# Attention units of 128 instead of 96 tokens, and a first MoE in six blocks of 512 tokens

## Chip, cores and metric

The kernel runs on one core of a Trainium2 chip. The metric is the device time of the kernel in microseconds. The core has a matrix engine (TensorE, PE in the profile; its weight loads are PEld), VectorE (DVE), ScalarE (ACT), GpSimd (POOL) and SyncE (SP), which here issues every DMA. TensorE writes to PSUM only; VectorE and ScalarE read PSUM.

## The reference, cut to what matters

A chunked attention is followed by two feed-forward layers, all in float32. Queries come in chunks of 32; a chunk sees 8 memory keys and a window from 16 keys before it to 8 keys behind it, which makes 64 keys.

```
# q, k, v: (4, 8 heads, 768, 64); mem_k, mem_v: (4, 8, 8, 64)
for c in range(24):
    k_full = concat([mem_k, k[max(0, 32*c - 16):min(768, 32*c + 40)]])
    v_full = concat([mem_v, v[same window]])
    scores = q[32*c:32*c + 32] @ k_full.T / 8
    a = exp(scores - max(scores)); a = a / (sum(a) + 1e-9)
    out[32*c:32*c + 32] = a @ v_full
x = out as (3072 tokens, 512)
x = relu(x @ w_in)**2 @ w_out                        # first MoE: 512 -> 2048 -> 512
x = (silu(x @ w_gate) * (x @ w_val)) @ w_out2        # second MoE: 512 -> 1536 -> 512
```

## The kernel before

**Attention** is computed in 32 units of 96 tokens (three chunks), all eight heads of a unit at once. `at_load` brings q and k of a unit, `at_scores` makes 24 matmuls of 64 keys by 32 queries, each in a tile of 64 rows and 32 columns of TensorE's array: two rows of tiles for two heads, three columns of tiles for the three chunks. The scores lie in PSUM (`abank`, rows of 72 columns, because the third chunk's 64 keys begin 8 further on). VectorE takes the maximum, ScalarE the exponentials and their sums, VectorE divides and turns the probabilities with 32x32 transposes into `pT` (the unit's 128 keys by 96 queries for each head). `at_pv` multiplies: for each head the unit's v (128 keys by 64 columns) is the weight and `pT` the moving operand of 96 columns; even heads write the lower 64 PSUM partitions, odd heads the upper, so neighbours use the two 64-column halves of the array. A float32 matmul appears in the trace as two instructions, each with a weight load of its own. `at_split_x` splits the result into a high and a low part (`x`).

**The first four units** have another path: they are needed before anything else can run. Their softmax subtracts the maximum first (`at_sub_0`), the turning is done by TensorE (`at_turn_0`, L199) and the products with v are small ones of a single chunk and head (`at_pv_0`, L217; 24 matmuls a unit, each of 32 columns).

**The first MoE** runs over blocks of tokens, `BLOCKS = (4, 4, 5, 5, 5, 5, 4)` units, so of 384 or 480 tokens. In a block there are 16 steps `f`. In a step TensorE makes the hidden tile (`hidden_pe`, 12 matmuls with 128x128 weights and the block's tokens as columns, L373: high x high, high x low and low x high over four slices of 128) and, two steps later, the projection (`project_pe`, L417, 12 matmuls again). Between them ScalarE and VectorE take the ReLU, square it twice and make its low part (`relu`, `square`, `square_again`, `square_lo`). Hidden tiles alternate between two PSUM banks. The order on TensorE is hidden(f+2), projection(f), hidden(f+3), projection(f+1), and so on.

**Where the other work stands** is fixed by tables. A step has four slots, so before there are 448. Everything up to the last two steps of the first block is written out in `OPENING`, a list of letters and unit or step numbers (S scores, T turning, O products with v, x y w v the pieces of the first hidden tile, a b hidden, c d projection, L weight loads). Behind that, `UNIT_AT` says at which slot a unit's products with v stand; its other stages stand `UNIT_LAGS` slots after the products of the unit before, in the order load, scores, maximum, two halves of the exponentials, normalization, turning, load of v, rest of the turning. `PREP_AT` and `PREP_LAGS` do the same for 18 chunks of weights of the second MoE, which pass through ScalarE, VectorE and GpSimd and go back to DRAM. Engines and the SP queue work in this order, and an instruction that waits holds what stands behind it on its engine.

**The second MoE** (L607, L654) runs over the tokens in blocks of 512 columns and is reached when the first is done. Its lines are not touched.

Of the kernel before, what the change touches and what calls it, by code (L numbers as in the profile page):

```python
# [19 lines left out]
GQ = 96  # L20
GK = 128
NG = S // GQ
NGRP = B * NG
NH = 8
# [4 lines left out]
UNIT_AT = (  # L29
    65, 76, 90, 101, 114, 126, 138, 151, 164, 178, 190, 203, 215, 227, 240, 254, 267, 279, 291, 305, 321, 337,  # L30
    353, 369,
)
UNIT_LAGS = (-8, 0, 1, 2, 5, 5, 6, 7, 5)
PREP_LAGS = (-11, 0, 2, 2, 4, 7, 6, 9, 10, 11)
BLOCKS = (4, 4, 5, 5, 5, 5, 4)
# [4 lines left out]
PREP_AT = (77, 102, 132, 146, 158, 178, 196, 212, 226, 238, 260, 270, 287, 300, 324, 340, 352, 364)  # L40
# [4 lines left out]
GM = GK + NMEM  # L45
UK = NI * GM
UCOLS = UQ + UK + UV
UV0 = 3 * NI * D
WN = 64
WK = 72  # L50
# [7 lines left out]
PIECES = (((0, 0), (32, 32)), ((0, 32), (32, 64)), ((0, 64), (32, 96), (64, 32)))  # L58
# [17 lines left out]
def attention_moe_moe_kernel(ctx, tc, att, v0, w1, w2, out):  # L76
# [39 lines left out]
    probs = [ap.tile([GQ, NH, GQ], F32, name=f"prob{i}") for i in range(2)]  # L116
    pT = ap.tile([128, NH, GQ], F32, name="pT")

    blk0 = [sum(BLOCKS[:t]) for t in range(len(BLOCKS))]
    units = [(t, g) for t, n in enumerate(BLOCKS) for g in range(blk0[t], blk0[t] + n)]  # L120
    xt = {}
    rows = []
    st = [dict() for _ in units]

    def at_load(u):
        t, g = units[u]
        if u in EARLY:
            raw = early[EARLY.index(u)][:, 0:UQ + UK]
        else:
            raw = ap.tile([128, UQ + UK], F32, tag="qk", name="qk")  # L130
        st[u]["raw"] = raw
        sp.dma_start(out=raw, in_=att[g, :, 0:UQ + UK])

    def at_load_v(u):
        t, g = units[u]
        if t:
            v = ap.tile([128, UV], F32, tag="v", name="v", bufs=2)
            sp.dma_start(out=v, in_=att[g, :, UQ + UK:])
        else:
            v = first_v[u // 2][:, u % 2 * UV0:(u % 2 + 1) * UV0]  # L140
            sp.dma_start(out=v, in_=v0[g])
        st[u]["v"] = v

    def at_scores(u):

        t, g = units[u]
        s = st[u]
        raw = s.pop("raw")
        wide = t > 0
        o = s["s"] = rows[1] if wide else rows[u % 2][:, :, :, 0:WN]  # L150
        for i in range(NI):
            for c in range(3):
                for r in range(2):
                    half = slice(64 * r, 64 * r + 64)
                    k = UQ + i * GM + (0, 32, 72)[c]
                    b = 8 if wide and c == 2 else 0
                    pe.matmul(  # L157
                        o[32 * c:32 * c + 32, r, i, b:b + 64],
                        raw[half, i * GQ + 32 * c:i * GQ + 32 * c + 32],
                        raw[half, k:k + 64], start=True, stop=True, tile_position=(64 * r, 32 * c),  # L160
                    )
        if g % NG == 0:
            dve.memset(o[0:32, :, :, 0:LEFT], NEG)
        if g % NG == NG - 1:
            e = 64 if wide else 64 - NMEM
            dve.memset(o[64:96, :, :, e - RIGHT:e], NEG)
# [5 lines left out]
    def at_sub_0(u):  # L172
# [7 lines left out]
        if u == BLOCKS[0] - 1:  # L180
            dve.memset(rows[1][64:96, :, :, 0:NMEM], NEG)
# [22 lines left out]
    def at_pv_0(u):  # L204
        t, g = units[u]
        s = st[u]
        if t not in xt:
            xt[t] = [xp.tile([128, KD, NTM], R, tag=f"x{i}", name=f"x{i}") for i in range(2)]
        v = s["v"].rearrange("p (c j d) -> p c j d", c=3, d=D)
        o = hbank[1][:, 0:KD * GQ].rearrange("p (j q) -> p j q", q=GQ)  # L210
        s["o"] = o.rearrange("p (r i) q -> p r i q", r=2)
        for j in range(NI):
            for c in range(3):
# [13 lines left out]
    def at_exp(u, heads=range(NH)):  # L227
# [29 lines left out]
    def at_turn(u, chunks=range(3)):  # L257
# [10 lines left out]
    def at_turn_2(u):  # L268
        at_turn(u, range(2, 3))

    def at_pv(u):
        t, g = units[u]
        s = st[u]
        if t not in xt:
            xt[t] = [xp.tile([128, KD, NTM], R, tag=f"x{i}", name=f"x{i}") for i in range(2)]
        o = s["o"] = abank[:, :, NI * WK:NI * WK + KD // 2 * GQ].rearrange("p r (i k) -> p r i k", k=GQ)
        for h in range(NH):
            r = D * (h % 2)
            pe.matmul(  # L279
                o[r:r + D, h // NI, h % NI // 2], s["v"][:, h * D:(h + 1) * D], pT[:, h],  # L280
                start=True, stop=True, tile_position=(0, r),
            )

    def at_x(u):
        t, g = units[u]
        c = (g - blk0[t]) * GQ
        return [x[:, :, c:c + GQ].rearrange("p (r i) k -> p r i k", r=2) for x in xt[t]]

    def at_x_hi(u):
        act.copy(at_x(u)[0], st[u]["o"])  # L290

    def at_x_lo(u):
        hi, lo = at_x(u)
        dve.tensor_tensor(lo, st[u]["o"], hi.bitcast(F32), ALU.subtract)
        st[u].clear()

    def at_split_x(u):
        at_x_hi(u)
        at_x_lo(u)
# [7 lines left out]
    nunit = BLOCKS[0]  # L307
    before = -1
    for t, n in enumerate(BLOCKS[1:], 1):
        for j in range(n):  # L310
            e = 13 * j + 12 if t == 1 else UNIT_AT[nunit - 8]
            for lag, fn in STAGES:
                plan.setdefault(max(0, before + lag + (t == 2 and j == 0 and lag > 2)), []).append((lag, fn, nunit))
            plan.setdefault(e, []).append((100, at_pv, nunit))
            plan.setdefault(e + 1, []).append((101, at_split_x, nunit))
            before = e
            nunit += 1
# [7 lines left out]
    nt_of = [GQ * n for n in BLOCKS]  # L325
# [96 lines left out]
    def project(t, f, between):  # L422
# [5 lines left out]
        if f == NF1 - 1:  # L428
            t0 = blk0[t] * GQ
# [275 lines left out]
    for i in range(2):  # L705
        pool.memset(probs[i][:, :, WK:GQ], 0.0)
    for o in (yb0, abank):
        rows.append(o[0:GQ, :, 0:NI * WK].rearrange("p r (i k) -> p r i k", k=WK))
    dve.memset(rows[1], NEG)
# [22 lines left out]
    def side(hs):  # L732
# [15 lines left out]
        "O": lambda u: (at_pv_0 if u < BLOCKS[0] else at_pv)(u), "X": at_x_hi, "Y": at_x_lo, "F": at_exp_1,  # L748
# [6 lines left out]
        "M": lambda u: (at_max_0 if u < BLOCKS[0] else at_max)(u),  # L755
# [5 lines left out]
    early = [t[:, c:c + WC] for t in (rawp.tile([128, RAW], F32, tag="raw", name="early") for _ in range(2)) for c in (0, WC)]  # L761
# [110 lines left out]
def _pack(inputs):  # L872
# [8 lines left out]
    att = np.empty((NGRP, 128, UCOLS), q.dtype)  # L881
    for b in range(B):
        for g in range(NG):
            w0 = g * GQ
            win_k = np.concatenate([kp[b, :, w0:w0 + CHUNK], mk[b], kp[b, :, w0 + CHUNK:w0 + GK - NMEM]], axis=1)
            win_k = np.concatenate([win_k, mk[b]], axis=1)
            win_v = np.concatenate([vp[b, :, w0:w0 + CHUNK], mv[b], vp[b, :, w0 + CHUNK:w0 + GK - NMEM]], axis=1)
            a = att[b * NG + g]
            qT = q[b, :, w0:w0 + GQ].reshape(2, NI, GQ, D).transpose(0, 3, 1, 2)
            kT = win_k.reshape(2, NI, GM, D).transpose(0, 3, 1, 2)  # L890
            a[:, 0:UQ] = qT.reshape(128, UQ)
            a[:, UQ:UQ + UK] = kT.reshape(128, UK)
            a[:, UQ + UK:] = win_v.transpose(1, 0, 2).reshape(GK, UV)
    v0 = np.empty((BLOCKS[0], 2, WN, 3, NI, D), v.dtype)
    for g in range(BLOCKS[0]):
        rows = att[g, :, UQ + UK:].reshape(GK, NI, 2, D)
        for c, keys in enumerate((rows[0:64], rows[32:96], np.concatenate([rows[72:128], rows[32:40]]))):
            v0[g, :, :, c] = keys.transpose(2, 0, 1, 3)
    v0 = v0.reshape(BLOCKS[0], 128, UV0)
# [38 lines left out]
```

## Time and profile before

| | |
|---|---|
| median of 3 runs | 1133.77 us (1133.75 to 1133.96) |
| the profiled execution | 1131.54 us |
| its span, first to last instruction | 1129.8 us |
| TensorE busy | 1116.8 us, 99% of the span |
| VectorE, ScalarE, GpSimd busy | 705.6, 532.5, 317.5 us |
| granted clock, mean | 0.999 |

The span is what the trace shows; 1.7 us of the execution lie outside it. Busy time is the union of an engine's instructions. Matmuls are pipelined, so a busy TensorE isn't TensorE at its peak; how fast its stream runs is read from the times between instructions, which the chain shows as pieces. Times in the trace are in us from the span's start, and the trace lacks a few records of TensorE.

### The profile page before, as it was taken

To read this page: it belongs to the slowest core of one execution; us is meant where nothing else is said; L and a number is where in the kernel's file an instruction comes from. 1 tells how busy PE (TensorE), PEld (TensorE's weight loads), DVE (VectorE), ACT (ScalarE), POOL (GpSimd) and SP (SyncE) were. 2 spreads that over 40 slices of the span, in tenths; PEclk is the share of its full clock that TensorE was granted. 3 is DMA by queue.
4 is the path that set the end of the run, shared out by engine and by line. 5 is a ranking of instruction groups with operands and counts; after the bars stand their busy time and mean duration, and the time that the engine had idled before them with its cause. 6 is when DMAs were issued, how large, how long until landed. Compare 5 with 4: busy or idle time off the path is not lost.

```text
span 1129.8 us, 18416 instructions
## 1 busy us (share of the span) xinstructions
PE 1116.8 (99%) x7160; PEld 966.3 (86%) x7160; DVE 705.6 (62%) x1059; ACT 532.5 (47%) x1212; POOL 317.5 (28%) x263
## 2 busy tenths in 40 slices
PE   6999999999999999999999999999999999999998
PEld 6999999888888888888999888888888888888887
DVE  7897655654555565545253666697666697666664
ACT  5996665565665656565462222352222253222242
POOL 0000230522244234145000332461332362332251
PEclk9999999999999999999999999999999999999999
DMA  9831445464654564545443664467557567655751
GB/s 378 322 127 43 142 156 197 152 198 149 192 181 156 171 216 138 190 144 178 151 149 111 253 227 157 165 216 242 186 191 272 203 210 226 204 191 202 256 224 56
DMA packets 72678, 212.47 MB, mean 188 GB/s; under 512 B 5648, under 2 KB 41488, under 8 KB 56336
## 3 DMA queue, kind: packets, MB, share of 16 engines
q1 hardware_dynamic: 72592, 211.31, 53.8%
q8 instruction: 56, 0.92, 0.3%
q14 instruction: 30, 0.25, 0.1%
HBM read 165.68 MB, written 45.61 MB: 187 GB/s over the span
## 4 chain that ended last, share of the span: by engine, by line
PE 99%; DVE 1%; DMA 0%; issue 0%; ACT 0%; ACTq 0%
PE hbank L373 24%; PE yb L417 24%; PE hbank L607 15%; PE yb L607 15%; PE abank L654 7%; PE yb L654 7%; PE abank L279 2%; PE abank L157 2%; PE hbank L217 1%; PE hbank L654 1%; DMA qk<-in_att_dram 0%; PE yb L199 0%; DVE first_p L177 0%; DVE mx L170 0%; PE yb L157 0%
## 5 line engine op out<-in xcount | busy, mean ns | idle before, releaser
L373 PE MATMUL hbank<-x,w 128*128 128x480 f32 (+3 forms) x1356 | 289.6, 361 | 0.0
L373 PEld LDWEIGHTS hbank<-x,w 128*128 128x128 f32 x1356 | 246.1, 189 | 23.7 <-issue 0.2
L417 PE MATMUL yb<-gh,w 128*128 128x480 f32 (+1 forms) x896 | 201.2, 361 | 0.0
L398 DVE TENSOR_TENSOR gl<-r,gh 128x480 fp32r<-128x480 f32 (+1 forms) x112 | 77.7, 695 | 190.2 <-ACT r L392 189.6
L417 PEld LDWEIGHTS yb<-gh,w 128*128 128x128 f32 x896 | 162.5, 188 | 15.8
L106 POOL TENSOR_TENSOR ring<-uf,ring 128x512 fp32r<-128x512 f32 x51 | 71.7, 1407 | 274.4 <-ACT ring L103 274.4
L472 POOL TENSOR_TENSOR wraw<-cut 128x256 f32<-128x256 f32 x36 | 27.3, 758 | 376.0 <-DVE cut L458 295.3
L607 PE MATMUL hbank<-w,wst 128*128 128x512 f32 x540 | 132.6, 389 | 0.0
L607 PE MATMUL yb<-w,wst 128*128 128x512 f32 x540 | 132.6, 389 | 0.0
L381 ACT ACTIVATE r<-hbank 128x480 f32<-128x480 f32 (+1 forms) x112 | 60.2, 538 | 132.4 <-PE hbank L373 132.2
L607 PEld LDWEIGHTS hbank<-w,wst 128*128 128x128 f32 x540 | 101.4, 188 | 21.1
L607 PEld LDWEIGHTS yb<-w,wst 128*128 128x128 f32 x540 | 101.3, 188 | 21.0
L417 PE MATMUL yb<-gl,w 128*128 128x480 f32 (+1 forms) x448 | 110.2, 359 | 0.0
L645 ACT ACTIVATE tmp<-tmp 128x512 f32<-128x512 f32 x36 | 22.8, 633 | 169.8 <-DVE tmp L644 169.8
L103 ACT CAST ring<-uf 128x512 fp32r<-128x512 f32 x108 | 67.1, 621 | 45.8 <-PE yb L654 21.0
L417 PEld LDWEIGHTS yb<-gl,w 128*128 128x128 f32 x448 | 82.1, 188 | 7.5
L594 POOL TENSOR_TENSOR uf<-uf 128x512 f32<-128x512 f32 x36 | 53.9, 1498 | 121.2 <-DVE uf L646 107.7
L260 DVE STREAM_TRANSPOSE pT<-prob 32x256 f32<-32x256 f32 x196 | 85.2, 435 | 3.2
L654 PE MATMUL abank<-ring,wst 128*128 128x512 f32 x360 | 83.3, 389 | 0.2 <-issue 0.2
L654 PE MATMUL yb<-ring,wst 128*128 128x512 f32 x360 | 83.3, 389 | 0.1
L233 ACT ACTIVATE prob<-abank,mx 96x72 f32<-96x72 f32 x224 | 67.7, 311 | 26.6 <-DVE mx L225 26.3
L654 PEld LDWEIGHTS abank<-ring,wst 128*128 128x128 f32 x360 | 67.5, 188 | 14.6 <-issue 0.6
(134 smaller groups left out, 1510.2 us busy)
## 6 DMA issues: line engine op xcount, KB each, us to landing
wst<-w2d SPq DMA_DIRECT2D x93, 1024.0 KB, 4.9
wraw<-in_w_dram SPq DMA_DIRECT2D x34, 1024.0 KB, 6.6
qk<-in_att_dram SPq DMA_DIRECT2D x28, 464.0 KB, 4.4
w2d<-wraw SPq DMA_DIRECT2D x48, 256.0 KB, 3.4
v<-in_att_dram SPq DMA_DIRECT2D x28, 256.0 KB, 4.7
w2d<-wraw SPq DMA_DIRECT2D x12, 512.0 KB, 4.1
zraw<-y1d SPq DMA_DIRECT2D x6, 1024.0 KB, 8.4
w2d<-head SPq DMA_DIRECT2D x18, 256.0 KB, 2.1
```

The source lines that it names most:

```text
L103: act.copy(hi, src)
L106: lo_engine.tensor_tensor(lo, src, hi.bitcast(F32), ALU.subtract)
L233: act.activation(probs[u % 2][:, h, 0:WK], s["s"][:, r, i], AF.Exp, bias=s["mx"][:, r, i:i + 1], scale=SCALE, accum_out=s["sm"][:, h],)
L260: dve.transpose(pT[row:row + 32, :, 32 * c:32 * c + 32], probs[u % 2][32 * c:32 * c + 32, :, col:col + 32],)
L373: pe.matmul(hbank[f % 2][:, cols], wt[:, k * 128:(k + 1) * 128], x[:, k, cols], start=i == 0, stop=i == 3 * KD - 1,)
L381: act.activation(r, hbank[f % 2][:, 0:n], AF.Relu)
L398: dve.tensor_tensor(gl, g["r"], g["gh"].bitcast(F32), ALU.subtract)
L417: pe.matmul(ybank[e][:, 0:nt_of[t]], wt[:, c:c + 128], gtile[t, f][g], start=f == 0 and p == 0, stop=f == NF1 - 1 and p == 2,)
L472: pool.tensor_tensor(o, x, y, op)
L594: pool.tensor_tensor(u_of(p, o), u_of(p, x), u_of(p, y), op)
L607: pe.matmul(to, wt[:, k * 128:k * 128 + 128], x[:, k], start=m == 0, stop=m == 5)
L654: pe.matmul(to[k], wt[:, 128 * k:128 * k + 128], u, start=p == 0 and m == 0, stop=p == NP - 1 and m == 2,)
```

## The change

A unit has four chunks (128 tokens), so 24 units instead of 32; scores are 32 matmuls and use all four columns of tiles, and rows are 64 columns wide. The keys of four chunks do not fit in 128 rows, so the products with v are made over two halves of 96 keys each, one for each pair of chunks: two matmuls of 64 columns for each head instead of one of 96. v comes from an array of its own (`av`), 384 KiB a unit instead of 256 KiB, into one buffer instead of two. q and k of a unit are 592 KiB instead of 464 KiB; two of the early ones land in buffers of `x`. The first MoE has six blocks of 512 tokens, four units each, and so 384 slots. The slot tables are new, and `OPENING` is the same list but for the places of O5 and d6.

```diff
-GQ = 96
-GK = 128
+NC = 4
+GQ = NC * CHUNK
+GK = 96
...
-UNIT_LAGS = (-8, 0, 1, 2, 5, 5, 6, 7, 5)
-PREP_LAGS = (-11, 0, 2, 2, 4, 7, 6, 9, 10, 11)
-BLOCKS = (4, 4, 5, 5, 5, 5, 4)
+UNIT_AT = (65, 81, 97, 113, 129, 145, 161, 177, 193, 209, 225, 241, 257, 273, 289, 305)
+UNIT_LAGS = (-8, 0, 2, 3, 5, 7, 8, 8, 10)
+PREP_LAGS = (-8, 0, 2, 3, 4, 6, 7, 8, 9, 10)
+BLOCKS = (512, 512, 512, 512, 512, 512)
...
+KAT = (0, 32, 72, 104)
+GM = KAT[-1] + 64
...
     def at_scores(u):
...
-            for c in range(3):
+            for c in range(NC):
...
-                    k = UQ + i * GM + (0, 32, 72)[c]
-                    b = 8 if wide and c == 2 else 0
+                    k = UQ + i * GM + KAT[c]
...
+    def at_turn(u, chunks):
         for c in chunks:
-            for col, row in PIECES[c]:
+            pair, row = divmod(32 * c, 64)
+            for k in (0, 32):
                 dve.transpose(
-                    pT[row:row + 32, :, 32 * c:32 * c + 32],
-                    probs[u % 2][32 * c:32 * c + 32, :, col:col + 32],
+                    pT[row + k:row + k + 32, pair, :, row:row + 32], probs[u % 2][32 * c:32 * c + 32, :, k:k + 32],
                 )
...
     def at_pv(u):
-        t, g = units[u]
         s = st[u]
+        v = s["v"].rearrange("p (n c) -> p n c", n=2)
+        o = s["o"] = abank[:, :, NI * WN:].rearrange("p r (i k) -> p r i k", k=GQ)
+        for h in range(NH):
+            r = D * (h % 2)
+            for n in range(2):
+                pe.matmul(
+                    o[r:r + D, h // NI, h % NI // 2, 64 * n:64 * n + 64], v[:, n, h * D:(h + 1) * D], pT[:, n, h],
+                    start=True, stop=True, tile_position=(0, r),
+                )
...
-            v = ap.tile([128, UV], F32, tag="v", name="v", bufs=2)
+            v = ap.tile([GK, 2 * UV], F32, tag="v", name="v", bufs=1)
```

On TensorE, at the very start, stand the scores (L157 before, L150 after), the turnings (L199, L189) and the products with v (L217, L204) of the first units, and the first pieces of the first hidden tile. A row gives line, output and inputs, the shape of one and how many. Before:

```order
L157 MATMUL yb_77<-early 32x64 x24
L199 MATMUL yb_78<-eye,first_p 128x96 x4
L157 MATMUL abank<-early 32x64 x24
L199 MATMUL yb_79<-eye,first_p 128x96 x4
L217 MATMUL hbank_75<-first_p,first_v 64x32 x48
L199 MATMUL yb_78<-eye,first_p 128x96 x4
L217 MATMUL hbank_75<-first_p,first_v 64x32 x24
L199 MATMUL yb_79<-eye,first_p 128x96 x4
L373 MATMUL hbank_74<-x_255,w 128x288 x4
L217 MATMUL hbank_75<-first_p,first_v 64x32 x24
```

After:

```order
L150 MATMUL yb_77<-early 32x64 x32
L189 MATMUL yb_78<-eye,first_p 128x128 x4
L150 MATMUL abank<-early 32x64 x32
L189 MATMUL yb_79<-eye,first_p 128x128 x4
L204 MATMUL hbank_75<-first_p,first_v 64x32 x64
L189 MATMUL yb_78<-eye,first_p 128x128 x4
L204 MATMUL hbank_75<-first_p,first_v 64x32 x32
L189 MATMUL yb_79<-eye,first_p 128x128 x4
L362 MATMUL hbank_74<-x_317,w 128x384 x4
L204 MATMUL hbank_75<-first_p,first_v 64x32 x32
```

The order is the same; the counts and the widths grow by a third.

Still on TensorE, in the first block, around the products with v of unit 5 (L279 before, L265 after) and the scores of unit 6, with the first MoE's matmuls beside them. Before:

```order
L417 MATMUL yb_77<-gl,w 128x384 x2
L417 MATMUL yb_78<-gl,w 128x384
L417 MATMUL yb_79<-gl,w 128x384
L279 MATMUL abank<-pT,v 64x96 x8
L157 MATMUL abank<-qk 32x64 x24
L373 MATMUL hbank_75<-x_255,w 128x384 x4
```

After:

```order
L150 MATMUL abank<-qk 32x64 x32
L406 MATMUL yb_77<-gl,w 128x512 x2
L406 MATMUL yb_78<-gl,w 128x512
L406 MATMUL yb_79<-gl,w 128x512
L362 MATMUL hbank_75<-x_317,w 128x512 x4
L362 MATMUL hbank_75<-x_318,w 128x512 x4
L265 MATMUL abank<-pT,v 64x64 x16
L362 MATMUL hbank_75<-x_317,w 128x512 x4
```

The scores of unit 6 come ahead of the products of unit 5, and a third of a projection and two thirds of a hidden tile lie between them. At every later unit the products and the next scores stand together, as before.

## Rows read from the trace of the kernel before

**Rows 1.** The page: busy time, and the chain that ended last by line.

```profile
PE 1116.8 (99%) x7160; PEld 966.3 (86%) x7160; DVE 705.6 (62%) x1059; ACT 532.5 (47%) x1212; POOL 317.5 (28%) x263
...
PE hbank L373 24%; PE yb L417 24%; PE hbank L607 15%; PE yb L607 15%; PE abank L654 7%; PE yb L654 7%; PE abank L279 2%; PE abank L157 2%; PE hbank L217 1%; PE hbank L654 1%; DMA qk<-in_att_dram 0%; PE yb L199 0%; DVE first_p L177 0%; DVE mx L170 0%; PE yb L157 0%
```

**Rows 2.** Groups of instructions by form, TensorE: count, busy us, mean ns.

```profile
L373 PE MATMUL hbank<-x,w 128*128 128x480 f32 x768 | 178.0, 379 | 0.0
L607 PE MATMUL hbank<-w,wst 128*128 128x512 f32 x540 | 132.6, 389 | 0.0
```

**Rows 3.** The chain, 500 to 615 us: start, length in us, what.

```profile
508.16 0.81 PE abank L279 x16
508.97 0.67 PE abank L157 x46
509.63 2.80 PE yb L417 x12
512.44 2.60 PE hbank L373 x12
...
544.12 2.08 PE hbank L373 x12
```

**Rows 4.** The chain, 611 to 625 us, second MoE.

```profile
613.97 2.72 PE yb L607 x12
```

**Rows 5.** TensorE's timeline in single windows of 5 ns: start, length, instructions running.

```profile
52.89 0.42 PE L279 MATMUL abank<-pT,v 128*64 128x96 f32 x6
...
52.97 0.42 PE L279 MATMUL abank<-pT,v 128*64 128x96 f32 x6
...
53.48 0.33 PE L157 MATMUL abank<-qk 64*32 64x64 f32 x12
...
53.48 0.44 PE L157 MATMUL abank<-qk 64*32 64x64 f32 x24
```

**Rows 6.** The chain, 0 to 120 us, opening.

```profile
0.81 3.51 DMA qk<-in_att_dram
...
4.36 1.15 PE yb L157 x48
...
10.54 0.87 PE yb L199 x4
...
13.27 2.73 PE hbank L217 x48
...
16.02 0.49 ACT x L290
...
16.53 0.57 DVE x L294
...
24.98 1.07 PE hbank L373 x4
...
31.03 7.15 PE hbank L373 x40
```

**Rows 7.** Stretches: length, busy us of each engine, granted clock, DMA share, GB/s.

```profile
0.00:31.00 31.00, 21.95 (x457) 19.30 (x457) 21.41 (x41) 17.35 (x24) 1.75 (x10) 1.00 0.95 382
31.00:130.00 99.00, 98.96 (x900) 96.03 (x896) 79.93 (x138) 78.68 (x202) 0.00 (x0) 1.00 0.44 163
130.00:540.00 410.00, 410.00 (x3140) 355.25 (x3139) 228.45 (x410) 246.38 (x676) 138.80 (x127) 1.00 0.51 170
```

**Rows 8.** Line L157: duration in ns, shortest, median, longest.

```profile
L157 PE MATMUL abank<-qk x1296: 216/216/240, 53.5 to 509.4; 64*32 64x64 f32 x186
...
L157 PE MATMUL yb<-qk x48: 310/311/313, 4.4 to 5.1; 64*32 64x64 f32 x48
```

**Rows 9.** Waits: who for whom, us in total, times, longest.

```profile
DVE gl L398 <- ACT r L392: 189.6, 75, 6.2
```

**Rows 10.** SP's own waits, and the page's DMA issues: KB, us to landing.

```profile
SPq L111 <- DMA w2d<-wraw: 20.0, 9, 4.1
...
v<-in_att_dram SPq DMA_DIRECT2D x28, 256.0 KB, 4.7
```

More of the change, by code (lines that the diff above doesn't have):

```diff
@@ L57 @@
 RAW = 2048
-PIECES = (((0, 0), (32, 32)), ((0, 32), (32, 64)), ((0, 64), (32, 96), (64, 32)))
 WC = 1024
@@ L115, in attention_moe_moe_kernel @@
     ap = actx.enter_context(tc.tile_pool(name="ap", bufs=1))
[L116 to L120, printed above, removed]
+    probs = [ap.tile([GQ, NH, WN], F32, name=f"prob{i}") for i in range(2)]
+    pT = ap.tile([GK, 2, NH, 64], F32, name="pT")
+    tok0 = [sum(BLOCKS[:t]) for t in range(len(BLOCKS) + 1)]
+    block_of = [max(t for t in range(len(BLOCKS)) if tok0[t] <= g * GQ) for g in range(NGRP)]
     xt = {}
     rows = []
-    st = [dict() for _ in units]
+    st = [dict() for _ in range(NGRP)]
     def at_load(u):
-        t, g = units[u]
         if u in EARLY:
@@ L131, in at_load @@
         st[u]["raw"] = raw
-        sp.dma_start(out=raw, in_=att[g, :, 0:UQ + UK])
+        sp.dma_start(out=raw, in_=att[u])
     def at_load_v(u):
-        t, g = units[u]
-        if t:
-            v = ap.tile([128, UV], F32, tag="v", name="v", bufs=2)
-            sp.dma_start(out=v, in_=att[g, :, UQ + UK:])
+        if u >= NU0:
+            v = ap.tile([GK, 2 * UV], F32, tag="v", name="v", bufs=1)
+            sp.dma_start(out=v, in_=av[u])
         else:
             v = first_v[u // 2][:, u % 2 * UV0:(u % 2 + 1) * UV0]
-            sp.dma_start(out=v, in_=v0[g])
+            sp.dma_start(out=v, in_=v0[u])
         st[u]["v"] = v
     def at_scores(u):
-        t, g = units[u]
         s = st[u]
         raw = s.pop("raw")
-        wide = t > 0
-        o = s["s"] = rows[1] if wide else rows[u % 2][:, :, :, 0:WN]
+        o = s["s"] = rows[u % 2 if u < NU0 else 1]
         for i in range(NI):
-            for c in range(3):
+            for c in range(NC):
                 for r in range(2):
                     half = slice(64 * r, 64 * r + 64)
-                    k = UQ + i * GM + (0, 32, 72)[c]
-                    b = 8 if wide and c == 2 else 0
+                    k = UQ + i * GM + KAT[c]
                     pe.matmul(
-                        o[32 * c:32 * c + 32, r, i, b:b + 64],
+                        o[32 * c:32 * c + 32, r, i],
                         raw[half, i * GQ + 32 * c:i * GQ + 32 * c + 32],
@@ L204, in at_pv_0 @@
     def at_pv_0(u):
-        t, g = units[u]
         s = st[u]
-        if t not in xt:
-            xt[t] = [xp.tile([128, KD, NTM], R, tag=f"x{i}", name=f"x{i}") for i in range(2)]
-        v = s["v"].rearrange("p (c j d) -> p c j d", c=3, d=D)
+        v = s["v"].rearrange("p (c j d) -> p c j d", c=NC, d=D)
         o = hbank[1][:, 0:KD * GQ].rearrange("p (j q) -> p j q", q=GQ)
@@ L212, in at_pv_0 @@
         for j in range(NI):
-            for c in range(3):
+            for c in range(NC):
                 q = slice(32 * c, 32 * c + 32)
@@ L268, in at_turn_2, with at_x, at_x_hi, at_x_lo @@
     def at_turn_2(u):
-        at_turn(u, range(2, 3))
+        at_turn(u, range(2, NC))
     def at_pv(u):
-        t, g = units[u]
         s = st[u]
+        v = s["v"].rearrange("p (n c) -> p n c", n=2)
[7 more added lines that the diff above has]
+                )
+    def at_x(u, part):
+        t = block_of[u] + part
         if t not in xt:
             xt[t] = [xp.tile([128, KD, NTM], R, tag=f"x{i}", name=f"x{i}") for i in range(2)]
[L276 to L299, printed above, removed]
+        a, b = max(u * GQ, tok0[t]), min(u * GQ + GQ, tok0[t + 1])
+        return [st[u]["o"][:, :, :, a - u * GQ:b - u * GQ]] + [
+            x[:, :, a - tok0[t]:b - tok0[t]].rearrange("p (r i) k -> p r i k", r=2) for x in xt[t]
+        ]
+    def at_x_hi(u, part=0):
+        o, hi, lo = at_x(u, part)
+        act.copy(hi, o)
+    def at_x_lo(u, part=0):
+        o, hi, lo = at_x(u, part)
+        dve.tensor_tensor(lo, o, hi.bitcast(F32), ALU.subtract)
+    def at_split_x(u, part=0):
+        at_x_hi(u, part)
+        at_x_lo(u, part)
     STAGES = tuple(zip(UNIT_LAGS, (
@@ L306, in attention_moe_moe_kernel @@
     plan = {}
[L307 to L317, printed above, removed]
+    before = 51
+    for u in range(NU1, NGRP):
+        e, t = UNIT_AT[u - NU1], block_of[u]
+        for lag, fn in STAGES:
+            plan.setdefault(before + lag + (u == NU1 and lag > 2), []).append((lag, fn, u))
+        plan.setdefault(e, []).append((100, at_pv, u))
+        plan.setdefault(e + 1, []).append((101, at_split_x, u))
+        if u * GQ + GQ > tok0[t + 1]:
+            plan.setdefault(QB * t - 8, []).append((102, lambda u: at_split_x(u, 1), u))
+        before = e
     def attention(hs):
@@ L324, in attention_moe_moe_kernel @@
     w = {}
-    nt_of = [GQ * n for n in BLOCKS]
+    nt_of = BLOCKS
     gtile = {}
@@ L704, in attention_moe_moe_kernel @@
     pool.memset(pT, 0.0)
-    for i in range(2):
-        pool.memset(probs[i][:, :, WK:GQ], 0.0)
     for o in (yb0, abank):
-        rows.append(o[0:GQ, :, 0:NI * WK].rearrange("p r (i k) -> p r i k", k=WK))
-    dve.memset(rows[1], NEG)
+        rows.append(o[:, :, 0:NI * WN].rearrange("p r (i k) -> p r i k", k=WN))
     wplan = {}
@@ L760, in attention_moe_moe_kernel @@
     }
-    early = [t[:, c:c + WC] for t in (rawp.tile([128, RAW], F32, tag="raw", name="early") for _ in range(2)) for c in (0, WC)]
+    early = [rawp.tile([128, RAW], F32, tag="raw", name="early") for _ in range(2)]
+    early += [xp.tile([128, KD * NTM], F32, tag=f"x{i}", name="early") for i in range(2)]
     first_v = [wp.tile([128, RAW], F32, tag="w", name="first_v") for _ in range(2)]
@@ L880, in _pack @@
     vp[:, :, LEFT:LEFT + S] = v
-    att = np.empty((NGRP, 128, UCOLS), q.dtype)
+    att = np.empty((NGRP, 128, UQ + UK), q.dtype)
+    av = np.empty((NGRP, GK, 2, UV), v.dtype)
     for b in range(B):
@@ L884, in _pack @@
             w0 = g * GQ
-            win_k = np.concatenate([kp[b, :, w0:w0 + CHUNK], mk[b], kp[b, :, w0 + CHUNK:w0 + GK - NMEM]], axis=1)
-            win_k = np.concatenate([win_k, mk[b]], axis=1)
-            win_v = np.concatenate([vp[b, :, w0:w0 + CHUNK], mv[b], vp[b, :, w0 + CHUNK:w0 + GK - NMEM]], axis=1)
+            parts = (kp[b, :, w0:w0 + 32], mk[b], kp[b, :, w0 + 32:w0 + 96], mk[b], kp[b, :, w0 + 96:w0 + 152])
             a = att[b * NG + g]
             qT = q[b, :, w0:w0 + GQ].reshape(2, NI, GQ, D).transpose(0, 3, 1, 2)
-            kT = win_k.reshape(2, NI, GM, D).transpose(0, 3, 1, 2)
+            kT = np.concatenate(parts, axis=1).reshape(2, NI, GM, D).transpose(0, 3, 1, 2)
             a[:, 0:UQ] = qT.reshape(128, UQ)
[L892 to L899, printed above, removed]
+            a[:, UQ:] = kT.reshape(128, UK)
+            for n in range(2):
+                c0 = w0 + 64 * n
+                keys = np.concatenate([vp[b, :, c0:c0 + 32], mv[b], vp[b, :, c0 + 32:c0 + 88]], axis=1)
+                av[b * NG + g, :, n] = keys.transpose(1, 0, 2).reshape(GK, UV)
+    av = av.reshape(NGRP, GK, 2 * UV)
+    v0 = np.empty((NU0, 2, WN, NC, NI, D), v.dtype)
+    for g in range(NU0):
+        for c in range(NC):
+            rows = av[g, 32 * (c % 2):32 * (c % 2) + WN, (c // 2) * UV:(c // 2 + 1) * UV].reshape(WN, NI, 2, D)
+            v0[g, :, :, c] = rows.transpose(2, 0, 1, 3)
+    v0 = v0.reshape(NU0, 128, UV0)
     wi, wo = inputs["moe_w_in"].view(np.int64), inputs["moe_w_out"].view(np.int64)
```

59 lines of the change are left out of this document (25 added, 34 removed).

## The prediction

> **What bounds the kernel now.** I read the page first. TensorE is busy for 1116.8 of 1129.8 us and the chain that ended last runs through its lines alone: 24% and 24% in the two halves of the first MoE (L373, L417), and 2% and 2% in the steady attention units (L279 the products with v, L157 the scores) [rows 1]. The reader is to see that 13.0 us of idle time is all that could be won by waiting less. So I next read what each piece of TensorE's work costs, and in which stage another engine could take its place.
>
> The chain gives the pace of the stream. Twelve matmuls take 2.60 us in a block of 480 tokens, 2.08 us in one of 384 [rows 3], and 2.72 us in the second MoE, whose matmuls all have 512 columns [rows 4]. Per matmul that is 216.7, 173.3 and 226.7 ns. Divided by the columns it is 0.451, 0.451 and 0.443 ns: 512 is the cheapest form per token. (The mean durations of one [rows 2] are latencies and overlap; the pace has to come from the chain.) An attention unit is 0.81 us of products with v, 0.67 us of scores, and the first twelve matmuls behind it take 2.80 instead of 2.60 us, so 0.20 us more for the switch [rows 3].
>
> In the opening the page's waits lie on the chain: the first load, VectorE's softmax of the first units, then TensorE's own small matmuls with two waits for a copy out of PSUM [rows 6]. TensorE also works at another speed there. Four matmuls of 288 columns take 1.07 us, 267 ns each, and a score instruction has a duration of 311 ns where it is later 216 [rows 6, 8]. The column of the granted clock reads 1.00 for that stretch [rows 7], but 288 columns and the 32 cycles that 384 and 512 columns also carry make 267 ns at 1.2 GHz, the lower of the two levels. I therefore price the opening from its own rows only.
>
> From 31 us on TensorE is busy throughout [rows 7]. VectorE has 79.9 of 99 us up to 130 us, and 228 of 410 us after; ScalarE 78.7 and 246.
>
> **The first MoE.** Before there are 7 blocks with 16 steps of 24 matmuls: 3 blocks of 384 tokens are 1152 matmuls at 173.3 ns, 199.7 us; 4 of 480 are 1536 at 216.7 ns, 332.8 us; together 532.5 us (the two shares of 24% are 541 us, with the switches and the slow first matmuls in them). After there are 6 blocks, 2304 matmuls of 512 columns at 226.7 ns: 522.2 us. That is **-10.3 us**. The price of 512 columns is from the second MoE; the matmuls there have the same 128x128 weights and the same type.
>
> **The steady units.** Before: 28 products with v (22.7 us), 27 sets of scores at this speed (18.1 us), 28 switches (5.6 us), 46.4 us. After there are 20, 19 and 21 (unit 5's products now stand apart from unit 6's scores, so one switch more).
> - Products with v: 16 instructions of 96 columns become 32 of 64. From below, by columns: 0.81 x 128/96 = 1.08 us. From above, by instructions: 1.62 us. The trace says which is nearer. Windows of 5 ns show that the oldest instruction still running started at 52.89 us in one window and at 52.97 in the next, with six in flight in both [rows 5]: a round of two instructions every 0.08 us, one in each 64-column half of the array, eight rounds for sixteen. 0.08 us is 192 cycles at 2.4 GHz for 96 columns, two for each: little is there that isn't columns. I take 1.08.
> - Scores: 48 instructions become 64, but the fourth chunk uses 32 columns of the array that stood empty. From below 0.67 us (rounds of eight instead of six), from above 0.89. The first 12 end after 0.33 us, 24 after 0.44 [rows 5], so a round of six costs 0.055 us; at that pace eight rounds would fit in 0.55, and the rest of the 0.67 must be the issue of instructions, which grows. I take the middle, 0.78.
> - After: 20 x 1.08 + 19 x 0.78 + 21 x 0.20 = 40.6 us. That is **-5.8 us**, between -7.9 and +7.1 at the bounds.
>
> The rule that speaks against this is in the Trainium skill, TensorE: Matmul & The Clock Gate, Part 3 (The mechanism): a weight load overlaps running matmuls only where the row group differs; both column halves here use all rows. With that page's load time (columns / 1.2 ns, 53 ns for 64) the 32 loads alone would be 1.71 us, an estimate, and the sum would turn from -9.7 to +2.9 us. The trace disagrees so far: sixteen instructions, each with its load, take 0.81 us with six in flight [rows 3, 5], where 53 ns for each load would already be 0.85.
>
> **The opening** serves four units of 128 tokens instead of 96, at the lower speed.
> - The products with v of the first units (L217) go from 48 to 64 instructions of the same shape. Four pieces of about 2.74 us [rows 6] become 3.66: +3.7.
> - The transposes on TensorE (L199) go from 96 to 128 columns, four pieces of about 0.84 us: +1.1.
> - Scores: three pieces on the chain, of which the first is 1.15 us [rows 6]; +0 if eight tiles run as six did, +1.1 by instructions; I take +0.3.
> - The first hidden tile: three groups of four matmuls go from 288 to 384 columns, 267 to 347 ns each, +1.0; twelve of 96 become 128. Of the 7.15 us of that piece [rows 6] 24 at 173.3 ns and four at 267 leave 1.9 us for these; a third at most, I take +0.3. The first term has counted 0.6 us of both already: +0.7.
> - The first load has 592 instead of 464 KiB; at the 382 GB/s of the opening [rows 7] that is +0.3. Split and copy out of PSUM (0.49 and 0.57 us [rows 6]) go from 384 to 512 columns: +0.35 in all.
> Sum **+6.4 us**, bounds 4.5 and 8.5. Weight loads queued behind the larger q and k loads on SP come later by some 3 us (five times 128 KiB, four times 128 KiB of v, at 382 GB/s), TensorE's need for them by 6, so they stay covered.
>
> **Edits costed at nothing.** VectorE's softmax steps are paid by columns, not partitions, and get narrower or stay (72 to 64 keys); transposes go from 7 to 8 per unit, 196 to 160 in all. A single v buffer: the load is issued 8 slots after the products that free it and 8 before the next ones, 8 x 1.36 = 10.9 us, against 4.7 us to land 256 KB now, 384 KB after [rows 10]. Sixteen units and 18 weight preparations now fill slots 65 to 311, 335 us at 1.36 us a slot; before it was slots 65 to 375, 63 at 1.04 and 247 at 1.30 us, 387 us. VectorE's share stays near 56% (fewer transposes and subtractions), ScalarE's goes from 60% to about two thirds, and each slot is longer for whoever is late. What hides them is the four groups of 2.72 us between a hidden tile and its projection; VectorE waits for ScalarE's squares 189.6 us in all [rows 9], so there is room.
>
> **Sum**: -10.3 - 5.8 + 6.4 = -9.7 us. The profiled execution took 1131.54 us with its span of 1129.8, 2.2 us under the median of the runs shown, 1133.77. So 1121.8 us for the profiled one and **1124.0** for the median. With the lower bounds of both terms it is 1120.1; with the scores at their upper bound (+2.1) and the opening at 8.5 it is 1128.2. That is the range of the likeliest case.
>
> **Rivals.**
> 1. The pairs are lost (slower). The two halves of a head follow one another in the same half of the array; before, neighbours alternated. If neighbours no longer overlap, 32 instructions run one behind the other at 0.055 us (two cycles for each of 64 columns, 0.053, and a little over), 1.76 us and 0.15 us around them, 1.91 us a unit: +16.6 us on my sum, 1140.6. It turns the gain into a loss above 1.08 + 9.7/20 = 1.57 us a unit. The rule above would end near here. Against it: scores with six tiles also emit two instructions per tile and still start in rounds of six. 6%; with the bound by instructions, 1.62 us a unit, 1134.8, another 4%.
> 2. No gain by width. If 512 columns in the first MoE cost 13/12 of their columns, as 384 and 480 do there, the first term is 0: 1134.3. Against it stand 2.72 us per twelve in all pieces of the second MoE. 5%. (The same page, Back-to-back issue gap, gives 2.5 ns over the columns per matmul, which would make the term -1.0 us; the rows have 13 ns and more.)
> 3. A new wait in the denser middle: a weight chunk's store holds SP, the next chunk's load is late, ScalarE's in-order queue waits with it and TensorE's hidden tile isn't drained. SP waited 20.0 us for such stores already [rows 10] and none reached TensorE. If each of the 18 chunks cost 0.3 us: +5.4, 1129.4. 10%.
> 4. The forecast: 75%.
>
> **Numbers.** About 0.2% (2.3 us) is what a measurement of this kernel can tell from no change. Faster holds the forecast and rival 3: 85%; same takes rival 2 and the milder half of rival 1: 9%; slower 6%. The range reaches from under the lower bounds to where the likeliest case and rival 3 end, 1119.5 to 1130; rivals 1 and 2, 15%, are left out.
>
> **What would show it.** In the profile after, twelve matmuls of the first MoE take 2.72 us and the second MoE begins some 10 us earlier; a steady unit reads about 1.08 and 0.78 us; the steady matmuls begin some 6 us later than 31 us; TensorE has no idle beyond the opening. Wrong would be a unit of more than 1.5 us for the products with v, 2.77 us per twelve, or waits of TensorE for ScalarE or VectorE after 60 us.

## The result, and the profile after

The changed kernel takes 1122.22 us (median of 4 runs, 1119.87 to 1122.80) against 1133.76 us of before on the same chip: a ratio of 0.990 with the interval 0.988 to 0.992. The forecast was 1124.0 with 1119.5 to 1130. The profiled execution took 1119.87 us, the shortest of the four, with a span of 1118.0, 11.8 us under the span of before; that one, too, lay 2.2 us under its median.

The page after, busy time and the chain by line (L362 and L406 are the first MoE, L265 and L150 the units, L204 the first units' products with v):

```profile
PE 1103.6 (99%) x7032; PEld 912.6 (82%) x7032; DVE 657.4 (59%) x955; ACT 506.0 (45%) x1026; POOL 316.0 (28%) x261
...
PE yb L406 24%; PE hbank L362 23%; PE yb L596 15%; PE hbank L596 15%; PE yb L643 7%; PE abank L643 7%; PE abank L265 2%; PE abank L150 1%; PE hbank L204 1%; PE hbank L643 1%; PE yb L189 0%; DVE ring L104 0%; DMA qk<-in_att_dram 0%; DVE first_p L169 0%; DVE mx L162 0%
```

As in [rows 1], TensorE is the chain; its idle time is 14.4 us, where it was 13.0. So the gain is busy time of TensorE (13.2 us less), not waiting that went away. The chain in the steady part, 160 to 210 us (start, length, what), answers to [rows 3]:

```profile
162.62 1.13 PE abank L265 x32
163.75 0.79 PE abank L150 x53
164.54 2.94 PE yb L406 x12
167.48 2.72 PE hbank L362 x12
```

Twelve matmuls take 2.72 us in the first MoE too, a unit 1.13 and 0.79 us, and the switch behind it 0.22 (2.94 instead of 2.72). The second MoE's second group, in the chain around 600 us, was at 613.97 [rows 4]:

```profile
601.94 2.72 PE yb L596 x12
```

It begins 12.0 us earlier; behind it the two traces run the same 516 us to within 0.3. The opening, chain from 0 to 60 us, answers to [rows 6]:

```profile
10.81 1.09 PE yb L189 x4
...
14.19 3.64 PE hbank L204 x64
...
19.22 3.63 PE hbank L204 x64
...
24.62 3.63 PE hbank L204 x64
...
30.58 2.04 PE hbank L204 x64
...
42.89 2.72 PE yb L406 x12
```

Three of the four products with v became a third longer, as their count did; the fourth is shorter than any was before. The first projection begins at 42.89 us, 4.7 us later than before. It is the mark that the experiments use: **what lies before it is the opening, what lies behind it the stream.** In stretches (length, busy us of PE, PEld, DVE, ACT, POOL, granted clock, DMA share, GB/s), against [rows 7]:

```profile
36.00:130.00 94.00, 94.00 (x767) 77.41 (x767) 68.91 (x109) 70.68 (x156) 0.00 (x0) 1.00 0.40 138
130.00:530.00 400.00, 400.00 (x3091) 329.86 (x3090) 190.75 (x341) 228.78 (x547) 136.37 (x127) 1.00 0.55 185
```

TensorE is busy throughout, VectorE at 48% and ScalarE at 57% of the denser middle, both below what was forecast. TensorE's waits (for whom, us, times, longest) hold nothing from the steady part of the first MoE:

```profile
PE hbank L204 <- DVE x L285: 1.4, 1, 1.4
PE hbank L204 <- ACT first_p L192: 0.7, 1, 0.7
PE hbank L362 <- ACT wraw L340: 0.7, 1, 0.7
PE yb L643 <- DVE sum L674: 0.4, 1, 0.4
```

The third is new and lies in the opening, at 35.9 us; the chain gives 0.69 us of it as "issue" (time in which the engine waited for nothing that the profile shows), and no other profile of this opening has it. The last is in the second MoE, at 918 us. The kernel before has no such wait; the prediction named waits for VectorE after 60 us as a sign of being wrong, and this is one, of 0.4 us.

### The profile page after: what moved, and what is told of

Read it like the earlier page. It is cut to its first block, busy times and chain, and to the rows that moved or that the text cites. A ratio compares the mean times of both kernels' runs of the same rounds, so it can differ in the third digit from the quotient of the medians.

```text
span 1118.0 us, 17869 instructions
## 1 busy us (share of the span) xinstructions
PE 1103.6 (99%) x7032; PEld 912.6 (82%) x7032; DVE 657.4 (59%) x955; ACT 506.0 (45%) x1026; POOL 316.0 (28%) x261
## 4 chain that ended last, share of the span: by engine, by line
PE 98%; DVE 1%; ACT 0%; DMA 0%; issue 0%; ACTq 0%
PE yb L406 24%; PE hbank L362 23%; PE yb L596 15%; PE hbank L596 15%; PE yb L643 7%; PE abank L643 7%; PE abank L265 2%; PE abank L150 1%; PE hbank L204 1%; PE hbank L643 1%; PE yb L189 0%; DVE ring L104 0%; DMA qk<-in_att_dram 0%; DVE first_p L169 0%; DVE mx L162 0%
## 5 line engine op out<-in xcount | busy, mean ns | idle before, releaser
L362 PE MATMUL hbank<-x,w 128*128 128x512 f32 (+2 forms) x1164 | 279.3, 389 | 0.7 <-ACT wraw L340 0.7
L362 PEld LDWEIGHTS hbank<-x,w 128*128 128x128 f32 x1164 | 217.6, 188 | 45.4 <-issue 0.9
L387 DVE TENSOR_TENSOR gl<-r,gh 128x512 fp32r<-128x512 f32 x96 | 75.8, 792 | 246.4 <-ACT r L381 246.4
L406 PE MATMUL yb<-gh,w 128*128 128x512 f32 x768 | 194.7, 392 | 0.0
L406 PEld LDWEIGHTS yb<-gh,w 128*128 128x128 f32 x768 | 143.0, 188 | 30.5
L370 ACT ACTIVATE r<-hbank 128x512 f32<-128x512 f32 x96 | 57.5, 599 | 159.0 <-PE hbank L362 159.0
L406 PE MATMUL yb<-gl,w 128*128 128x512 f32 x384 | 105.7, 390 | 0.0
L406 PEld LDWEIGHTS yb<-gl,w 128*128 128x128 f32 x384 | 72.0, 188 | 15.0
L643 PEld LDWEIGHTS yb<-ring,wst 128*128 128x128 f32 x360 | 67.5, 188 | 14.8 <-ACT w L101 0.8
L248 DVE STREAM_TRANSPOSE pT<-prob 32x256 f32<-32x256 f32 x160 | 69.5, 435 | 2.3
```

The costliest lines, as they stand in the source:

```text
L248: dve.transpose(pT[row + k:row + k + 32, pair, :, row:row + 32], probs[u % 2][32 * c:32 * c + 32, :, k:k + 32],)
L362: pe.matmul(hbank[f % 2][:, cols], wt[:, k * 128:(k + 1) * 128], x[:, k, cols], start=i == 0, stop=i == 3 * KD - 1,)
L370: act.activation(r, hbank[f % 2][:, 0:n], AF.Relu)
L387: dve.tensor_tensor(gl, g["r"], g["gh"].bitcast(F32), ALU.subtract)
L406: pe.matmul(ybank[e][:, 0:nt_of[t]], wt[:, c:c + 128], gtile[t, f][g], start=f == 0 and p == 0, stop=f == NF1 - 1 and p == 2,)
L643: pe.matmul(to[k], wt[:, 128 * k:128 * k + 128], u, start=p == 0 and m == 0, stop=p == NP - 1 and m == 2,)
```

## Experiments

The theory: time is the sum of TensorE's pieces, the stream behind the first projection is fixed, and the opening depends on when TensorE comes to full pace. Rivals were a gain that comes from fewer units and not from width, a fixed price per matmul, halves of the array that do not overlap, and a first profile that was lucky. The times below are medians. The kernel before, measured again beside them, took 1133.38 us for the first four experiments, 1133.29 for the four with extra matmuls and 1133.93 for the last two.

**The changed kernel again**, no edit.

> The changed kernel, unchanged. Theory: the time is the sum of TensorE's pieces, so from the first projection on every piece has the same length (2.72 us per twelve matmuls, 1.13 and 0.79 us a unit), and executions differ by when TensorE reaches its full pace in the opening: the first projection begins at 42.9 us in the first profile, later in a slower one, and the span differs by the same amount. Rival: they differ in the second MoE, where the first profile has a wait of some 0.4 us.

Measured: 1122.54 us (1120.28 to 1123.20), profile with a span of 1118.3. The opening in its chain:

```profile
14.33 2.23 PE hbank L204 x64
...
18.00 3.52 PE hbank L204 x64
...
23.29 3.63 PE hbank L204 x64
...
29.25 3.56 PE hbank L204 x64
...
43.14 2.72 PE yb L406 x12
```

Now the first of the four is the short one. In this execution the profile has the granted clock of the opening itself (the number ahead of the DMA share):

```profile
14.00:17.00 3.00, 2.53 (x66) 2.16 (x64) 2.48 (x7) 1.56 (x4) 0.00 (x0) 1.00 1.02 415
17.00:20.00 3.00, 2.00 (x41) 2.03 (x42) 2.60 (x4) 3.00 (x5) 0.00 (x0) 0.70 0.99 404
20.00:34.00 14.00, 13.27 (x173) 12.07 (x170) 8.71 (x12) 8.30 (x11) 0.00 (x0) 0.50 1.02 421
...
36.00:44.00 8.00, 8.00 (x43) 6.89 (x43) 6.91 (x12) 6.88 (x23) 0.00 (x0) 1.00 1.02 327
```

At 1.00 (2.4 GHz) 64 small matmuls take 2.0 to 2.2 us, at 0.50 (1.2 GHz) 3.5 to 3.6. That shows what the prediction read from durations alone. Ahead of 14 us the column reads 1.00 as well, but the turnings at 11 and 13 us take 1.09 and 1.04 us, as at the low pace (0.63 us in the run warm_early_v below), so there it can't be trusted. The stream is the same: 1118.3 - 43.14 is 1075.2 us, 1118.0 - 42.89 is 1075.1. The rival is out: the wait in the second MoE is in both. Both profiles are of the shortest execution of their set; that a longer one has the same stream is seen only in the next kernels.

**The loops over heads and halves exchanged.**

```diff
-        for h in range(NH):
-            r = D * (h % 2)
-            for n in range(2):
+        for n in range(2):
+            for h in range(NH):
+                r = D * (h % 2)
                 pe.matmul(
```

> Products with v with the loops exchanged: all eight heads for the first 96 keys, then for the second, so that neighbours alternate between the two 64-column halves of the array. Theory: TensorE overlaps the halves whatever stands first, 1.13 us a unit stays, time as the changed kernel within 1 us. Rival (two products in a row in one half cost overlap): 1.05 us or less a unit, 1.6 us or more in all.

Measured: 1121.47 us (1119.88 to 1124.14), too wide a spread for 1 us. The chain decides:

```profile
215.00 1.08 PE abank L265 x32
216.08 0.79 PE abank L150 x53
```

1.08 instead of 1.13 us, between the theory's 1.13 and the rival's 1.05. The rival has a point, but a small one: 0.05 us a unit, 1.0 us in all, which is about the stream's difference too (1122.0 - 47.80 is 1074.2 us). Halves overlap in either order. This profile also shows the dearest opening of all, 4.9 us more than in the first one, in a kernel whose opening is the same:

```profile
37.17 10.63 PE hbank L362 x40
47.80 2.72 PE yb L406 x12
```

**Units of 128 tokens with seven blocks.**

```diff
-UNIT_AT = (65, 81, 97, 113, 129, 145, 161, 177, 193, 209, 225, 241, 257, 273, 289, 305)
+UNIT_AT = (65, 85, 105, 129, 149, 169, 193, 213, 233, 257, 277, 297, 321, 337, 353, 369)
-BLOCKS = (512, 512, 512, 512, 512, 512)
+BLOCKS = (512, 512, 384, 384, 384, 384, 512)
-PREP_AT = (71, 82, 93, 104, 115, 135, 146, 157, 168, 179, 199, 211, 223, 237, 263, 275, 287, 301)
+PREP_AT = (77, 102, 135, 146, 158, 178, 199, 212, 226, 238, 263, 275, 287, 301, 327, 340, 352, 364)
```

> Units of 128 tokens, but the first MoE in seven blocks of 512, 512, 384, 384, 384, 384 and 512 tokens, slots of the units and preparations spread accordingly. Theory (price by form): 1152 matmuls at 226.7 ns and 1536 at 173.3 are 527.4 us against 522.2: 5.1 us slower than the changed kernel, 2.08 us per twelve in the narrow blocks. Rival (the gain came from fewer units and their places, not from the width): within 1 us of the changed kernel.

Measured: 1126.88 us (1126.66 to 1127.39), a ratio of 0.994 (0.993 to 0.996) to before: 4.3 us over the changed kernel. The chain has both prices side by side:

```profile
214.90 2.72 PE hbank L362 x12
...
236.40 2.08 PE hbank L362 x12
```

The stream, 1125.1 - 44.65 = 1080.4 us, is 5.3 us longer than in six blocks; 5.1 was worked out. So the width is worth what its pieces say, and the rival (fewer units alone) is out. The opening is that of the changed kernel; here all four products with v ran at the low pace (3.56 to 3.63 us):

```profile
30.67 3.56 PE hbank L204 x64
...
36.92 7.73 PE hbank L362 x40
44.65 2.72 PE yb L406 x12
```

**The kernel before with eight blocks of 384 tokens.**

```diff
-BLOCKS = (4, 4, 5, 5, 5, 5, 4)
+BLOCKS = (4, 4, 4, 4, 4, 4, 4, 4)
-    65, 76, 90, 101, 114, 126, 138, 151, 164, 178, 190, 203, 215, 227, 240, 254, 267, 279, 291, 305, 321, 337,
-    353, 369,
+    65, 81, 97, 113, 129, 145, 161, 177, 193, 209, 225, 241, 257, 273, 289, 305, 321, 337, 353, 369, 385, 401,
+    417, 433,
```

> The kernel before with eight blocks of 384 tokens (four units of 96 each, 16 slots apart). Theory (price by form as read, 173.3 ns for 384 columns, 216.7 for 480): 3072 matmuls at 173.3 are 532.4 us against 532.5, so the time of before within 1 us. Rival (a fixed part of 13 ns for each matmul, whatever its width): 384 more matmuls cost 5.1 us.

Measured: 1135.33 us, 1.002 (1.001 to 1.003) of before, 2.0 us more. The waits and the chain at 260 us have most of it:

```profile
PE yb L417 <- DVE ys L433: 1.6, 1, 1.6
```

```profile
259.36 4.10 DMA w2d<-wraw
...
263.55 0.49 ACT ys L432
...
264.06 0.57 DVE ys L433
...
264.68 2.35 PE yb L417 x12
```

At one block's end the copy of the result needs a buffer that a weight chunk's store to DRAM still reads; the projection of the next block waits 1.6 us for it. The opening is that of the kernel before, yet the first projection begins later (TensorE's timeline: start, length, what):

```profile
30.97 10.46 PE L373 MATMUL hbank<-x,w 128*128 128x288 f32 x40
41.27 1.55 PE L417 MATMUL yb<-gh,w 128*128 128x384 f32 x8
```

So the stream is 1135.1 - 41.27 = 1093.8 us, 2.2 us over before (1129.8 - 38.18 = 1091.6); without the wait 0.6. 384 more matmuls cost 0.6 us and not 5.1: the price goes by form, 480 columns are no cheaper per column than 384, and the fixed price per matmul is out for these two. The wait is of the kind of the prediction's rival 3 (a weight chunk's store at its start), in another kernel.

**Extra matmuls in the opening.** They work on a constant and nobody reads what they write; the reference's computation is complete. Of the list only the places that change are shown.

```diff
+    hot = ap.tile([128, 512], mybir.dt.bfloat16, name="hot")
+    dve.memset(hot, 1.0)
+
+    def warm(n):
+        for _ in range(n):
+            pe.matmul(hbank[0], hot[:, 0:128], hot, start=True, stop=True)
...
-Q0 S0 M0 D0 Q1 S1 M1 D1 Q2 S2 E0
+Q0 H8 S0 M0 D0 Q1 S1 M1 D1 Q2 S2 H4 E0
...
-V0 O0 X0 L2
+V0 O0 H3 X0 L2
...
+        "H": warm,
```

> The changed kernel with 15 extra matmuls of 512 columns in bfloat16 on constants, into a PSUM bank that nothing uses yet: eight while TensorE waits for the first load, four while it waits for the first normalization, three while it waits for the split of unit 0. Theory: the opening is priced by the lower level of TensorE's clock; where it rises earlier, the products with v of the first units take about 2.0 us instead of 3.6 (as the fourth did in the first profile after), the first projection begins at 38 to 41 us instead of 42.9 to 47.8, and the time is 1118 to 1120.5 us with less spread. Rival: the small matmuls of the opening do not hold the pace, it falls back as it did at 18 us in the second profile, and the time stays within 1.5 us of 1122.4.

> As warm_start, with 8, 5, 4 and 2 extra matmuls, the last two where TensorE waits for the copy that the third unit's products need. Theory: the fewer gaps, the surer the early pace: at or under warm_start, first projection at 38 to 41 us. Rival: extra matmuls at the lower pace lie in the way (0.43 us each): later than warm_start by 1 us or more.

> The kernel before with the same 8, 5, 4 and 2 extra matmuls. Theory: the change's gain is the stream (-10.3 us) and the units (-4 to -5 us) less a dearer opening; with both openings at full pace the opening's term shrinks to 1 to 2 us, so this kernel is 1129 to 1132 us and the changed one with the same matmuls 12 to 14 us faster. Rival: the gain of the first profile (11.8 us) came in part from an early rise of the clock by chance; then the difference with both openings warm is 10 us or less.

> The changed kernel with the extra matmuls of warm_more and the loop order of pv_alternate. Theory: both gains add: 1.0 us (20 units by 0.05 us) under warm_more. Rival: the 0.05 us a unit is taken back by a later stage: equal to warm_more.

Measured: 1122.39 us (1117.76 to 1123.87) with 8, 4 and 3; 1119.60 (1118.67 to 1122.57) with 8, 5, 4 and 2; 1133.32 (1132.81 to 1134.76) for the kernel before; 1120.62 (1119.11 to 1121.22) with the exchanged loops. The first of these missed its 1118 to 1120.5 and fits its rival; its profile is of the shortest of seven executions. In the second, warm_more, the stretches show how far the pace held (granted clock ahead of the DMA share):

```profile
20.00:24.00 4.00, 2.99 (x68) 2.41 (x68) 3.45 (x7) 3.25 (x5) 0.00 (x0) 1.00 1.02 415
24.00:28.00 4.00, 3.78 (x32) 3.24 (x32) 2.72 (x4) 2.80 (x4) 0.00 (x0) 0.53 1.04 432
```

Its chain and its waits:

```profile
21.71 2.02 PE hbank L204 x62
...
26.97 3.56 PE hbank L204 x64
...
41.52 2.72 PE yb L406 x12
```

```profile
PE hbank L204 <- DMA first_v<-in_v_dram: 2.0, 3, 0.8
```

Both sides have a part. At full pace the first products do take 2.0 us, but then TensorE arrives before the loads of v do and waits 2.0 us for them, and behind 24 us the granted clock is down again, so the fourth unit's products take 3.56 us. So the theory's size (38 to 41 us for the first projection) is reached in one profile only (40.61 in warm_start, 41.52, and 44.27 in warm_alternate). For the kernel before nothing was won (its first projection begins at 39.48 us, 1.3 us later than without them): the expectation of 1129 to 1132 us missed. The difference between the two kernels with the same extra matmuls is 13.7 us, inside the 12 to 14 expected, but not by the reason given, since neither opening stayed at the full pace. That the first profile was not the source of the gain is shown by the streams and by the medians without extra matmuls (1133.38 and 1122.54 us). The exchanged loops were to win 1.0 us on warm_more; the stream did, the median did not, since in the profile the opening is 2.8 us longer. Streams: 1075.1 (warm_start), 1075.1 (warm_more), 1074.1 (warm_alternate), and 1091.6 us for the kernel before with them, each equal to its kernel without.

**The loads of v moved ahead**, with the extra matmuls and the exchanged loops; then four more extra ones.

```diff
-Q3 S3 L0 p0 T1
+Q3 S3 L0 V0 p0 T1
...
-V0 O0 X0 L2 Y0 V1 O1
+V1 O0 H4 X0 L2 V2 Y0 V3 O1
...
-E3 A3 V2 z2
+E3 A3 z2
...
-T3 V3 X2 x0
+T3 X2 x0
```

The second kernel has `T3 X2 H4 x0` there.

> As warm_alternate, and the four loads of v of the first units stand earlier in the opening: the first two behind the first weight load, the other two behind the second, instead of one behind each weight load. Theory: at full pace TensorE waits 2.0 us for these loads (warm_more), and the waits let the clock fall; without them the products with v of all four units run at 2.0 us, the first projection begins under 41 us and the time is 1117 to 1119.5 us. Rival: the weight loads that come 1 to 2 us later are then the wait (hidden tile of step 1), or the clock falls all the same because small matmuls do not hold it: 1119.5 to 1122 as warm_more and warm_alternate.

> As warm_early_v with four more extra matmuls between the turning of unit 3 and the first hidden tile. Theory (it is full-width work that holds the clock): no fall behind 24 us, 1 us under warm_early_v although the four cost 0.9 us at full pace. Rival: the clock falls earlier or not at all there, and the four cost their 0.9 to 1.7 us.

Measured: 1118.33 us (1117.57 to 1118.56), 0.986 (0.985 to 0.988) of before, and 1118.17 us (1118.11 to 1119.97). The waits for v shrink in the first:

```profile
PE hbank L195 <- DMA first_v<-in_v_dram: 0.5, 1, 0.5
```

and its chain still has the low pace from the third unit on (L195 is L204 there; the first piece is the second unit's):

```profile
18.47 1.94 PE hbank L195 x59
...
22.26 3.56 PE hbank L195 x64
...
42.05 2.72 PE yb L397 x12
```

The time is in the theory's range, its reason only half: the waits are down to 0.5 us, the clock falls all the same, and the first projection begins at 42.05 us, not under 41. Four more full-width matmuls did not keep the clock from falling (granted 0.50 from 21 to 30 us); the fourth unit's products come down to 2.31 us, the four cost as much, and there is no difference: the 1 us expected of them is not there. These are the two best versions, some 4 us under the changed kernel and 15.6 under before.

## Why the prediction held, point by point

**The stream** came out close to the sum of its terms. Behind the first projection the kernel before takes 1091.6 us in two profiles (one of them with extra matmuls), the changed one 1075.1 or 1075.2 in four (two of them with extra matmuls): 16.5 us less. By the terms: blocks -10.3, and -1.9 more since three hidden tiles lie ahead of the mark and grew by 0.64 us each; units 20 x 1.13 + 19 x 0.79 + 21 x 0.22 = 42.2 us against 28 x 0.81 + 27 x 0.67 + 28 x 0.21 = 46.7 (the switch before is 0.20 in blocks of 480 tokens and 0.22 in those of 384), -4.5. Together -16.7; the other 0.2 us is the second MoE, which got that much longer.
- The first MoE: 2.72 us per twelve, -10.3 us, shown in the chain, by the seven blocks (+5.3 for +5.1) and, for 480 against 384, by the eight. Rival 2 is out.
- The units: forecast -5.8, measured -4.5. Products with v were mis-sized, 1.13 instead of 1.08 us; the exchanged loops run at 1.08, so the 0.05 us is the order of the halves, the one grain of truth in rival 1. Scores were 0.79 for 0.78, the switch 0.22 for 0.20.
- The rule of the Trainium skill (TensorE: Matmul & The Clock Gate, Part 3, The mechanism), by which loads of weights for the same rows would not overlap with matmuls, does not hold here: 32 instructions, each with a load, end in 1.13 us, where that page's load time alone gives an estimate of 1.71. The measurement decides. (The same section of the Trainium skill also lets a load into a background weight buffer go ahead, which the prediction left out; no run here shows whether these loads do that.)
- The denser middle of the first MoE cost nothing, as forecast; rival 3 did not occur in this kernel. The 0.4 us wait in the second MoE was not foreseen. It is in every profile with six blocks and in none with seven or eight; why was not tested.

**The opening** was the term that was mis-sized. Forecast +6.4 us, measured 42.89 - 38.18 = 4.7 less the 1.9 that the blocks' term holds: +2.8 in the two first profiles. The pieces at the low pace grew as worked out (0.9 us for each of three products with v, 0.2 for a turning, 1.29 for 1.07 us of the hidden tile; scores hardly). What the step missed is that the pace of a piece isn't fixed: one of the four products ran at full pace in each profile of the changed kernel (another one each time), some 1.5 us less than priced.

Two pairs of profiles compare like with like. With all four products at the low pace in both, the seven blocks against the kernel before, the first projection begins 44.65 - 38.18 = 6.5 us later, which is +4.6. With a late rise of the clock in both, the exchanged loops against the eight blocks, it is 47.80 - 41.27 = 6.5 us and +4.6 again. Most of what is left to 6.4 is the first hidden tile: priced at +0.7, it gave -0.8 in the first pair, since the last 40 matmuls went only from 7.15 to 7.73 us, although the two tiles of twelve in them alone grow by 1.3: some of the others ran faster than before.

The medians of 1122.5 and 1133.4 us, less 1.8 outside the span and less the streams, leave openings of 45.6 and 40.0 us: +3.7. So the term is +3 to +5, by how the clock goes. This term (2.7 under the forecast) and the units (1.3 over) miss in opposite directions and make 1.4 of the forecast's error of 1.8 us; the rest is less than the spread of the runs. That the sum came so near is in part luck, and so is about 1 us of the 11.8 between the two first profiles, as the medians of the larger sets differ by 10.8.

What stays open is what makes the clock rise at one place of the opening or another; the runs show that it does, not why.

## What to carry to other kernels

Where one engine is busy 99% of the span, read the price of its pieces by form from the chain, not from mean durations: here the pieces added up to the measured gain of the stream to 0.2 us in 16. Divide a profile at the first steady piece: behind it two executions of one kernel agreed to 0.1 us, ahead of it profiles of the same opening differed by 5 us, and a change of the opening has to be judged on several executions. A faster opening can uncover the load behind it, as the loads of v here, so look at that load in the same step.

## What the runs showed of the hardware that was not expected

- TensorE was busy for 13.3 of the 14 us from 20 to 34 us in the second profile of the changed kernel and was granted 0.50 throughout; its work there was tiles of 64x64, turnings and a few wider matmuls. From 14 to 17 us, in work of the same kind, and from 36 us on it had 1.00.
- 480 columns cost 216.7 ns a matmul, 0.451 ns a column like 384 (173.3 ns), 512 only 0.443 (226.7 ns). With a fixed part as in the other two, 480 would take 213.3 ns.
- 32 instructions (16 matmuls) in column halves of the array take 1.13 us where two matmuls of one half follow each other, 1.08 us where the halves alternate.
